# A fused attention and MLP kernel: two bf16 dummy products fewer in the head, and q's transposing transfers issued directly behind x's

## The chip, the cores and the metric

The kernel runs on one core of a Trainium2 chip. A core has five engines that run side by side, each with its own queue that it works off in order: PE (TensorE, matrix products), DVE (VectorE), ACT (ScalarE), POOL (GpSimd) and SP (SyncE, which here only issues transfers). Data moves between the chip's memory and the core's working memory (SBUF) by transfers that run on 16 DMA engines; in this kernel SP, POOL and, at the very end, ACT issue them. Products are written to PSUM, of which there are eight banks. The metric is the device time of one execution in microseconds (us). Where a row of the profile says PEld, it is PE loading the stationary operand of a product.

## The reference

The inputs are q, k and v of shape (8, 8, 576, 64), that is 8 batches of 8 heads, 576 rows and 64 columns; a scale of 64 numbers; and two weight matrices. All are float32.

```python
kv = np.einsum('bhsd,bhse->bhde', k, v)
out = np.einsum('bhsd,bhde->bhse', q, kv)
rms = np.sqrt(np.mean(out * out, axis=-1, keepdims=True) + 1e-06)
attn = out / rms * g_norm
x = attn.transpose(0, 2, 1, 3).reshape(4608, 512)
h = x @ w_in                        # 512 -> 2048
g = np.where(h > 0.0, h, np.exp(np.minimum(h, 0.0)) - 1.0)
return g @ w_out                    # 2048 -> 512
```

It is an attention without softmax: one 64x64 matrix kv per head and batch, a product of q with it, and a normalisation of each row. An MLP with the ELU function follows. The result is float32 of shape (4608, 512).

## The kernel before

**Tiling.** The rows are worked in nine pieces T. Pieces 0 to 7 take the first 512 rows of each batch; piece 8 takes the last 64 rows of all eight batches. Each piece has an attention part, which makes x (512 rows, stored with the model dimension on the partitions, `xT`), and an MLP part. The MLP has two halves: `mm1(T, i)` for i = 0 to 7 makes two 128-wide strips of h with eight 128x512 products (line 466), and ACT and DVE turn them into `gT` (lines 478 to 497); `mm2(T, j, f0, f1)` makes a part of the output for a quarter j of the rows (line 513), ACT copies it to `o_sb` (line 526), and SP stores two quarters at a time (line 535).

**Order.** The order of work on each engine is the order in which the program is written; nothing reorders it. Where an instruction needs another engine's result it waits, and whatever is behind it on its engine waits too.

**The head (lines 550 to 761).** Before the first MLP can run, batch 0 goes through attention with a path of its own. `idle(ps, n, dtype)` (line 599) issues n products of a block of zeros into a PSUM bank that nobody reads: dummy products. They stand in four places: two in float32 and one in bf16 at the start (lines 609 and 610), one in float32 behind the first transposes of q (line 633), and one in bf16 between the score products and the kv products of the third and fourth quarter of the heads (line 729). Behind them come, quarter by quarter, kv (`kv_first`, line 174), scores (`se_first`, line 653), squares on ACT (line 662), their mean by a product with a constant matrix (`mean_first`, line 665), logarithm and exponential on ACT (lines 668 and 671), and a scaling on DVE (`scale_first`, line 674). `first` (line 683) then starts the first MLP on the quarters that are ready. k, v, both weight matrices and most of q are loaded by POOL's queue, with the cast to bf16 in the transfer (lines 104, 118, 136 and 142).

**The groups (function `group`, line 832).** From piece 2 on, the loop at line 900 runs one group per piece T. It holds the MLP's first half of piece T, pieces of the second half of T - 1, and the attention of T + 1. In step i = 0 stands kv of T + 1, in step 3 the scores, in step 4 (for T = 2: in steps 2 and 4) the scaled rows `xs`, and for each half of them a transposing transfer on SP, `xd0` and `xd1` (line 325), which writes x. A last scaling by g, `xg0` and `xg1` (line 332), runs on DVE in steps 6 and 7 (for T = 2: 5 and 6). The first product of the next group reads x.

**The q path.** For pieces 2 to 8, q also has to be transposed. The steps for a batch b are: `fetch(b)` (line 821) issues on POOL the loads of q, k and v; POOL unpacks q into `q_bf` by four copies (line 150), the last of which waits for v to land (line 132); then SP issues one transposing transfer from `q_bf` to `qT`, called `qd` (`q_dma`, line 251, issue in line 255). Before POOL fetches the batch after next, it runs a one-element copy, `landed` (lines 124 and 428), that waits until qT has landed; in the profile this is `gate<-qT` in line 125. So group T starts with `landed` of T + 1 and `fetch(T + 2)`, and its last statement is `ahead["qd"]()` for T + 2. For batch 2 and batch 3 `qd` is called ahead of the loop (lines 811 and 878). Piece 8 has its q loaded by SP (line 89) and cast by POOL.

So SP's order in a group from T = 3 on is: store, `xd0`, `xd1`, store, `qd`. Tiles for `qT`, `q_bf`, packed q, k and v exist twice, `o_sb` three times.

Of the kernel before, what the change touches and what calls it, by code (L numbers as in the profile page):

```python
# [16 lines left out]
def kernel(  # L17
# [16 lines left out]
    B, H, S, D = q.shape  # L34
# [8 lines left out]
    NT = B + 1  # L43
# [401 lines left out]
    def mm1(T, i, cols=(slice(0, 512),), relu=False, home="m1", between=(), by_c=False):  # L445

        if i == 0:
            gT[T] = mlpg.tile([P, FC, G], BF16, name="gT", tag="gT")
        x = xT[T]
        if home == "m2":  # L450
            h_ps = [ps_m2.tile([P, G], FP32, name="h_ps", tag="mm2") for _ in range(2)]
            parts = [(a, a + 1, h_ps[a].rearrange("p (a t) -> p a t", a=1)) for a in range(2)]
        else:
            if home == "at":
                both = at_tile(FP32).rearrange("p (a t) -> p a t", a=2)
            else:
                both = ps_m1.tile([P, 2, G], FP32, name="h_ps", tag="mm1")
            h_ps = [both[:, a, :] for a in range(2)]
            parts = [(0, 2, both)]
        for cs in cols:  # L460
            steps = [(a, c) for a in range(2) for c in range(KC)]
            if by_c:
                steps.sort(key=lambda step: step[1])
            for a, c in steps:
                f = 2 * i + a
                nc.tensor.matmul(  # L466
                    h_ps[a][:, cs],
                    lhsT=w_in_sb[:, c, f * P : f * P + P],
                    rhs=x(c, cs),
                    start=(c == 0),  # L470
                    stop=(c == KC - 1),
                )
        return elu(T, i, parts, relu, between)
# [34 lines left out]
    def mm2(T, j, f0, f1, hold=False):  # L508

        if f0 == 0 and (T, j) not in o_ps:  # L510
            o_ps[T, j] = ps_m2.tile([P, DM], FP32, name="o_ps", tag="mm2")
        for f in range(f0, f1):
            nc.tensor.matmul(  # L513
                o_ps[T, j],
                lhsT=gT[T][:, f, j * P : j * P + P],
                rhs=w_out_sb[:, f, :],
                start=(f == 0),
                stop=(f == FC - 1),
            )
        if f1 == FC and not hold:  # L520
            mm2_out(T, j)
# [74 lines left out]
    def bank(n):  # L596
        return ps_head.tile([P, G], FP32, name=f"bank{n}", tag=f"bank{n}")

    def idle(ps, n, dtype=BF16):
        z = zeros.bitcast(dtype)  # L600
        for _ in range(n):
            nc.tensor.matmul(ps, lhsT=z[:, 0:P], rhs=z[:, 0:512], start=True, stop=True)
# [4 lines left out]

    idle_ps = bank(1)
    idle(idle_ps, 2, FP32)
    idle(idle_ps, 1)  # L610
    q_st = q_raw0.rearrange("p u (l s j d) -> p u s j l d", l=2, s=2, j=J)
    q_two = attp.tile([P, NPAIR, J, 2, D], BF16, name="q_two", tag="q_two", bufs=1)
    qT0 = attp.tile([P, NPAIR, G], BF16, name="qT", tag="qT")
# [29 lines left out]
    def kv_first(c):  # L643
        u, l = c // 2, c % 2
        kv_single(0, kv_ps, u, (l,))
        ls = slice(l * 64, l * 64 + 64)
        nc.vector.tensor_copy(out=kv0[ls, u], in_=kv_ps[ls, :, u * 64 : u * 64 + 64])
# [19 lines left out]
    def log_first(c):  # L667
        nc.scalar.activation(r0[c], mean0[c], AF.Ln, bias=eps_col)
# [4 lines left out]
    def scale_first(c):  # L673
        nc.vector.scalar_tensor_tensor(
            out=x0[:, c, :], in0=se0[c], scalar=g_col, in1=r0[c], op0=ALU.mult, op1=ALU.mult
        )
# [43 lines left out]
    mean0[1] = bank(0)  # L720
    mean_first(1)
    log_first(1)
    idle_ps = bank(3)
    se0[2] = bank(1)
    se_first(2)
    square_first(2)
    exp_first(1)
    scale_first(0)
    idle(idle_ps, 1)
    kv_first(3)  # L730
    mean0[2] = bank(2)
    mean_first(2)
# [33 lines left out]
    at, ahead = attention(1), attention(2)  # L766
# [54 lines left out]
    def fetch(b):  # L821
        if b < B:
            fetch_packed_q(b)
            packed_kv(b)
            for name in "kv":
                fetch_packed_kv(name, b)
            unpack_q(b, Q)
        else:
            fetch_q(B)
            cast_q(B, Q)  # L830

    def group(T, at, lead, second, relu=()):

        for piece in lead:
            mm2(T - 1, *piece)
        if T == 2:
            for i in range(8):
                n = i // 2 - 1
                early = [at[f"sum{n}"], at[f"inv{n}"]] if i in (2, 4) else ()
                rest = mm1(T, i, relu=i in relu, between=early)  # L840
                for piece in second.get(i, ()):
                    mm2(T - 1, *piece)
                if i in (2, 4):
                    at[f"mul{n}"]()
                rest()
                if i in (2, 4):
                    at[f"xd{n}"]()
                if i == 0:
                    at["kv"]()
                if i in (1, 3):  # L850
                    at["se"]({i // 2: None})
                    at[f"sq{i // 2}"]()
                if i in (5, 6):
                    at[f"xg{i - 5}"]()
            return
        for i in range(8):
            between = [at["sq1"], at["sum0"], at["inv0"], at["sum1"]] if at and i == 4 else ()
            rest = mm1(T, i, relu=i in relu, between=between)
            if at and i == 3:
                at["se"]({0: None, 1: [ps_m2.tile([P, DM], FP32, name="se_ps", tag="mm2") for _ in range(2)]})  # L860
                at["sq0"]()
            for piece in second.get(i, ()):
                mm2(T - 1, *piece)
            if at and i == 4:
                at["inv1"]()
                for n in range(2):
                    at[f"mul{n}"]()
                    at[f"xd{n}"]()
            rest()
            if at and i == 0:  # L870
                at["kv"]()
            if at and i > 5:
                at[f"xg{i - 6}"]()

# [2 lines left out]
    at, ahead = ahead, attention(3)  # L877
# [22 lines left out]
    for T in range(2, NT):  # L900
        at = ahead if T + 1 < NT else None
        if T + 2 < NT:
            at["landed"]()
            fetch(T + 2)
            ahead = attention(T + 2)
        if T == 2:
            lead, pieces, steps = [], [(2 + i // 4, 4 * (i % 4), 4 * (i % 4) + 4) for i in range(2, 8)], range(1, 7)
        elif T < B:
            lead, pieces, steps = halves[:1], halves[1:], (0, 1, 2, 4, 5, 6, 7)
        else:  # L910
            lead, pieces, steps = halves[:1], halves[1:], range(7)
        second = {i: [piece] for i, piece in zip(steps, pieces)}
        group(T, at, lead, second, {2: (1, 2, 4, 5), B: ()}.get(T, (4, 5)))
        if T + 2 < NT:
            ahead["qd"]()
    rows = out.rearrange("(i l s) f -> l s i f", l=2, s=S)
    pieces = [(j, slice(0, DM)) for j in range(J - 1)]
# [46 lines left out]
```

## Time and profile before

Four runs of the kernel took 283.79 to 284.12 us, with a median of 283.96 us.

| | |
|---|---|
| time of the profiled execution | 283.96 us |
| its span, first to last instruction | 282.2 us |
| PE busy | 275.0 us (97%) |
| DVE busy | 161.7 us (57%) |
| ACT busy | 152.9 us (54%) |
| POOL busy | 58.5 us (21%) |
| mean granted clock of PE | 0.998 |
| transfers issued by SP and ACT, share of the 16 DMA engines | 24.2% |
| transfers issued by POOL, share of the 16 DMA engines | 40.5% |
| line 325, x's transposing transfers | 12, landing 3.2 us after issue |
| line 255, q's transposing transfers | 7, landing 4.5 us after issue |
| line 125, POOL's waits for qT | 6, 60.9 us in all |

How to read it: the span is the stretch that the profiler covers, and the run's time has some 1.8 us around it. A row of the timeline has the start, the length, the engine, the line of the kernel, the operation, what it writes and reads, how many instructions are merged into it, and in brackets how long the engine stood idle before it and what released it. The end of a product in a row is modelled, so products overlap in the rows; the distance between their starts is the time that they take. `SPq` rows are SP issuing transfers.

### The profile page before, as it was taken

The page shows a single profiled execution, that of the slowest core. Times are in us where ns is not written, and L with a number is a line of the kernel's source. Part 1 is how long each engine was busy: PE and PEld are TensorE (multiplying, and loading weights), DVE is VectorE, ACT ScalarE, POOL GpSimd, SP SyncE. Part 2 cuts the span into 40 slices and gives each one's busy share as a digit, 9 for nine tenths or more (in the row PEclk, how much of TensorE's full clock was granted, in tenths as well). Part 3 has the DMA queues.
Part 4 walks back from the last instruction along what each step waited for, and adds up shares of the span by engine and source line. Part 5 has one row for each costly group of instructions (what it writes and reads, how often), then busy time and mean ns, then how long its engine had stood idle before and what let it go on. Part 6 is the DMA issues. An engine that isn't in the chain of part 4 may idle for free.

```text
span 282.2 us, 5134 instructions
## 1 busy us (share of the span) xinstructions
PE 275.0 (97%) x2118; PEld 129.3 (46%) x2118; DVE 161.7 (57%) x233; ACT 152.9 (54%) x220; POOL 58.5 (21%) x102
## 2 busy tenths in 40 slices
PE   7799999999999999999999999999999999999994
PEld 3434554445444444444444444444444444444444
DVE  3449643988388646843693468445854586444400
ACT  3669446666487438533863377237923692333311
POOL 7843722152421241005110421012000000000000
PEclk9999999999999999999999999999999999999999
DMA  7999999696996695358945794354236123010122
GB/s 195 198 200 202 206 202 194 177 189 108 200 178 90 153 188 129 74 149 123 195 78 145 96 222 79 110 125 142 53 95 77 74 41 111 0 74 2 75 74 74
DMA packets 57579, 35.98 MB, mean 128 GB/s; under 512 B 32852, under 2 KB 55124, under 8 KB 57556
## 3 DMA queue, kind: packets, MB, share of 16 engines
q0 software_dynamic: 21808, 17.30, 40.5%
q1 hardware_dynamic: 35348, 17.83, 24.2%
q10 hardware_dynamic: 400, 0.52, 0.6%
q8 instruction: 16, 0.26, 0.4%
q14 instruction: 7, 0.06, 0.1%
HBM read 36.70 MB, written 9.44 MB: 164 GB/s over the span
## 4 chain that ended last, share of the span: by engine, by line
PE 92%; DMA 5%; POOL 1%; ACT 0%; issue 0%; DVE 0%; POOLq 0%
PE h_ps L466 42%; PE o_ps L513 39%; PE o_ps L923 5%; DMA w_in_sb<-in_moe_w_in_dram 3%; DMA k_pk<-in_k_dram 2%; PE at L174 2%; PE at L466 1%; PE at L200 1%; PE bank L683 1%; POOL w_in_sb L136 1%; PE se_ps L200 1%; ACT qT L248 0%; PE at L184 0%; PE se_ps L412 0%; DVE qT L249 0%
## 5 line engine op out<-in xcount | busy, mean ns | idle before, releaser
L466 PE MATMUL h_ps<-xT,w_in_sb 128*128 128x512 bf16 x536 | 125.7, 379 | 0.0
L513 PE MATMUL o_ps<-w_out_sb,gT 128*128 128x512 bf16 x512 | 120.5, 379 | 0.0
L478 ACT ACTIVATE elu_e<-h_ps 128x1024 bf16<-128x1024 f32 (+1 forms) x71 | 70.0, 995 | 80.6 <-PE h_ps L466 77.8
L466 PEld LDWEIGHTS <-w_in_sb 128*128 128x128 bf16 x552 | 52.5, 98 | 63.2 <-DVE xT L332 1.7
L513 PEld LDWEIGHTS <-gT 128*128 128x128 bf16 x512 | 49.5, 98 | 58.3
L489 DVE TENSOR_SCALAR elu_e<-elu_e 128x1024 bf16<-128x1024 bf16 (+1 forms) x75 | 33.1, 441 | 73.8 <-ACT elu_e L478 73.8
L497 DVE TENSOR_TENSOR gT<-elu_e,h_ps 128x1024 bf16<-128x1024 bf16 (+1 forms) x51 | 60.1, 1179 | 5.3
L526 ACT COPY o_sb<-o_ps 128x512 f32<-128x512 f32 x32 | 18.6, 586 | 15.5 <-PE o_ps L513 15.5
L217 DVE TENSOR_REDUCE ss<-sq 128x16 f32<-128x1024 bf16 x16 | 19.4, 1219 | 7.6 <-ACT sq L212 6.9
L150 POOL COPY q_bf<-q_pk 128x512 bf16<-128x512 bf16 x28 | 17.0, 637 | 23.7 <-DMA q_pk<-in_q_dram 23.7
L484 ACT ACTIVATE elu_h<-h_ps 128x1024 bf16<-128x1024 f32 (+1 forms) x20 | 19.5, 990 | 0.0
L497 DVE TENSOR_TENSOR gT<-elu_e,elu_h 128x1024 bf16<-128x1024 bf16 x20 | 14.1, 703 | 2.3 <-ACT elu_h L484 0.8
L923 PE MATMUL o_ps<-w_out_sb,gT 128*128 128x512 bf16 (+1 forms) x80 | 14.1, 337 | 0.0
L125 POOL COPY gate<-qT 1x1 bf16<-1x1 bf16 x6 | 1.1, 182 | 60.9 <-DMA qT<-q_bf 60.9
L104 POOL DMA_DIRECT2D q_pk<-in_q_dram x14 | 10.6, 758 | 4.0 <-issue 1.8
L228 DVE TENSOR_TENSOR xs<-at,ss 128x512 bf16<-128x512 f32 x16 | 10.2, 682 | 1.2 <-ACT ss L224 1.2
L923 PEld LDWEIGHTS <-gT 128*128 128x128 bf16 x80 | 7.7, 98 | 6.4 <-DVE gT L497 0.4
L212 ACT ACTIVATE sq<-at 128x1024 bf16<-128x1024 f32 x9 | 9.4, 1043 | 1.6 <-PE at L200 1.0
L118 POOL DMA_DIRECT2D k_pk<-in_k_dram x12 | 8.3, 691 | 3.1 <-DMA w_in_sb<-in_moe_w_in_dram 1.5
L118 POOL DMA_DIRECT2D v_pk<-in_v_dram x12 | 8.2, 684 | 2.9 <-DMA w_out_sb<-in_moe_w_out_dram 1.8
L174 PEld LDWEIGHTS <-k_pk 64*64 64x64 bf16 x576 | 6.5, 107 | 5.1 <-issue 4.6
L931 ACT COPY o_last<-o_ps 128x512 f32<-128x512 f32 (+1 forms) x5 | 2.5, 501 | 10.8 <-PE o_ps L923 10.8
(79 smaller groups left out, 138.6 us busy)
## 6 DMA issues: line engine op xcount, KB each, us to landing
out_dram<-o_sb SPq DMA_DIRECT2D x16, 512.0 KB, 3.8
q_pk<-in_q_dram POOLq DMA_DIRECT2D x14, 256.0 KB, 5.5
k_pk<-in_k_dram POOLq DMA_DIRECT2D x6, 576.0 KB, 8.5
v_pk<-in_v_dram POOLq DMA_DIRECT2D x6, 576.0 KB, 11.4
w_in_sb<-in_moe_w_in_dram POOLq DMA_DIRECT2D x5, 256.0 KB, 8.5
st_q<-in_q_dram SPq DMA_DIRECT2D x2, 512.0 KB, 5.5
w_out_sb<-in_moe_w_out_dram POOLq DMA_DIRECT2D x2, 512.0 KB, 13.7
w_out_sb<-in_moe_w_out_dram POOLq DMA_DIRECT2D x4, 256.0 KB, 11.3
```

The lines of the kernel that those rows point to most:

```text
L118: nc.gpsimd.dma_start(out=raw[name, b].rearrange("p h j d -> p h (j d)")[:, hs], in_=in_[:, hs])
L150: eng.tensor_copy(out=out_, in_=in_)
L174: nc.tensor.matmul(kv_ps[l * 64 : l * 64 + 64, s, u * 64 : u * 64 + 64], lhsT=bf["k", T][rows, j, 2 * u + l, :], rhs=bf["v", T][rows, j, 2 ...
L217: nc.vector.reduce_sum(out=ss, in_=sq.rearrange("p c (h e) -> p (c h) e", h=H), axis=AX.X)
L466: nc.tensor.matmul(h_ps[a][:, cs], lhsT=w_in_sb[:, c, f * P : f * P + P], rhs=x(c, cs), start=(c == 0), stop=(c == KC - 1),)
L478: nc.scalar.activation(e[:, lo:hi, :], ps, AF.Exp)
L484: nc.scalar.activation(h[:, lo:hi, :], ps, AF.Relu)
L489: nc.vector.tensor_scalar(out=e[:, lo:hi, :], in0=e[:, lo:hi, :], scalar1=1.0, scalar2=1.0, op0=ALU.min, op1=ALU.subtract,)
L497: nc.vector.tensor_tensor(out=gT[T][:, 2 * i + lo : 2 * i + hi, :], in0=e[:, lo:hi, :], in1=h, op=ALU.add if relu else ALU.max,)
L513: nc.tensor.matmul(o_ps[T, j], lhsT=gT[T][:, f, j * P : j * P + P], rhs=w_out_sb[:, f, :], start=(f == 0), stop=(f == FC - 1),)
L526: nc.scalar.copy(o_sb[T][:, j % 2, :], o_ps.pop((T, j)))
L923: nc.tensor.matmul(ps, lhsT=gT[B][:, f, j * P : j * P + P], rhs=w_out_sb[:, f, cols], start=(f == 0), stop=(f == FC - 1),)
```

## The change

Two calls of `idle` are taken out, each one bf16 product of 128x128 by 128x512 zeros: the third dummy at the start, and the one in front of the last quarter's kv, together with the PSUM bank that it was written to. The float32 dummies stay.

The call of `qd` at the end of a group stays only for T = 6, where T + 2 is piece 8. For the groups T = 2 to 5 it moves into `group`, behind step 5, so that the transfer for batch T + 2 is issued behind `xd1` of step 4. SP's order in these groups becomes: store, `xd0`, `xd1`, `qd`, store. The calls for batches 2 and 3 ahead of the loop are as before. The order of POOL, DVE and ACT is unchanged.

```diff
     idle_ps = bank(1)
     idle(idle_ps, 2, FP32)
-    idle(idle_ps, 1)
     q_st = q_raw0.rearrange("p u (l s j d) -> p u s j l d", l=2, s=2, j=J)
...
     log_first(1)
-    idle_ps = bank(3)
     se0[2] = bank(1)
     se_first(2)
     square_first(2)
     exp_first(1)
     scale_first(0)
-    idle(idle_ps, 1)
     kv_first(3)
...
                 if i == 0:
                     at["kv"]()
+                if i == 5:
+                    ahead["qd"]()
                 if i in (1, 3):
...
             rest()
             if at and i == 0:
                 at["kv"]()
+            if i == 5 and T + 2 < B:
+                ahead["qd"]()
             if at and i > 5:
                 at[f"xg{i - 6}"]()
...
         group(T, at, lead, second, {2: (1, 2, 4, 5), B: ()}.get(T, (4, 5)))
-        if T + 2 < NT:
+        if T + 2 == B:
             ahead["qd"]()
```

## The prediction

> **What bounds the kernel now.** I read the page first, then the chain that ended last, then the timeline of the head, and last the timelines of SP and POOL around the transfers that move.
>
> The page says that TensorE is the only full engine:
>
> ```profile
> span 282.2 us, 5134 instructions
> ...
> PE 275.0 (97%) x2118; PEld 129.3 (46%) x2118; DVE 161.7 (57%) x233; ACT 152.9 (54%) x220; POOL 58.5 (21%) x102
> ```
>
> The chain, in order of time, says from when it is full. Before 17.48 us the chain is a transfer, w_in_sb; behind it, up to 278.58, there are PE rows with one exception, two evacuations of qT at 33.26:
>
> ```profile
> 8.92 8.51 DMA w_in_sb<-in_moe_w_in_dram
> 17.43 0.05 issue
> 17.48 0.82 PE bank L683 x3
> ...
> 264.66 13.92 PE o_ps L923 x80
> ```
>
> So the time is "third chunk of w_in landed" + "products behind it" + a tail of stores. An edit counts only if it moves 17.48, or makes a gap in PE behind it. Seven L683 products take 1.51 us in the chain, 0.216 each.
>
> The timeline of the head holds both removed products, each the 128x512 bf16 kind:
>
> ```profile
> 4.94 0.38 PE L602 MATMUL bank<-zeros 128*128 128x512 bf16 x1
> ```
>
> ```profile
> 4.97 0.62 PEld L621 LDWEIGHTS <-q_two 128*128 128x128 bf16 x8 [0.61 <-DVE q_two L150]
> ...
> 7.91 0.47 PE L174 MATMUL kv_ps<-v_pk,k_pk 64*64 64x64 bf16 x18 [0.92 <-DMA v_pk<-in_v_dram]
> ...
> 12.12 0.39 PE L602 MATMUL bank<-zeros 128*128 128x512 bf16 x1
> 12.44 0.36 PEld L174 LDWEIGHTS <-k_pk 64*64 64x64 bf16 x18 [0.23 <-issue]
> ...
> 13.12 0.38 PE L665 MATMUL bank<-sq,means 128*128 128x512 bf16 x1 [0.21 <-ACT sq L662]
> ...
> 16.65 0.75 DVE L674 SCALAR_TENSOR_TENSOR xT<-bank,g_col,r 128x512 bf16<-128x512 f32 x1 [0.64 <-ACT r L671]
> ```
>
> And the end of the group that runs batch 3's MLP, where SP and DVE meet:
>
> ```profile
> 114.03 2.61 SPq L325 DMA_TRANSPOSE xT<-xs  x2
> ...
> 121.85 0.34 SPq L535 DMA_DIRECT2D out_dram<-o_sb  x1
> 122.24 0.48 DVE L332 TENSOR_SCALAR xT<-xT,g_col 128x1024 bf16<-128x1024 bf16 x1
> 122.28 2.58 SPq L255 DMA_TRANSPOSE qT<-q_bf  x1
> 122.77 1.41 PEld L466 LDWEIGHTS <-w_in_sb 128*128 128x128 bf16 x8 [0.34 <-DVE xT L332]
> ...
> 126.83 0.18 POOL L125 COPY gate<-qT 1x1 bf16<-1x1 bf16 x1 [17.07 <-DMA qT<-q_bf]
> ```
>
> L332 ends at 122.72 and the next group's first product starts at 122.78: the one place in a group where PE has no reserve.
>
> **The change, part by part.** *First dummy product* (0.22 us: 4.94 to 5.16). Without it the transposes start when their cast lets them, 4.97 plus some 0.1, so about 0.1 us earlier. The cover is the landing of v_pk: PE waits 0.92 us for it and starts kv at 7.91, whatever came before. Nothing.
>
> *Second dummy product* (0.32 us: 12.12 to 12.44). kv of the last quarter starts up to 0.32 earlier. What is late next is ACT: the mean product of 13.12 waits for a square that ACT ends at 13.07, and ACT is 100% busy from 11 to 15 us in the windows. The following cast on DVE (12.96) can start only when the scaling of 11.98 to 12.73 is done, so the score product of 13.43 gains 0.1 at most, and its square waits for ACT until 14.12 all the same. The first L683 product (13.76) waits for w_in. Then 17.43 stands. Nothing; were the cover gone it would be 0.32.
>
> *Four transposing q transfers* (batches 4 to 7; the call for batch 3 ahead of the loop and that for batch 8 stay). On SP each is 2.6 us of issue, and goes from behind one store of o_sb to ahead of it, directly behind x's second half. Does it wait there, with the store queued behind it? It needs q_bf: POOL's last copies end at 87.53, 109.76, 142.18 and 171.46; x's second issue ends at 88.81, 116.64, 146.20 and 174.93. It is ready by 1.3 to 6.9 us, more where the fetch comes earlier. The store of 121.85 finds SP free at 119.3; that of 91.06 waits until about 91.5, with three o_sb buffers behind it. Nothing.
>
> x's halves land 3.2 us after issue: the second, issued at about 115.35, at 118.5, and L332 takes it at 122.24. Were its remaining 1.9 us doubled by q's packets, 120.4: still in time. In batch 2's group the second half is issued about 87.55, lands at 90.7, at worst 92.6; L332 would end at 93.1, and PE wants it at 93.65. Nothing.
>
> The gate on POOL opens with qT's landing, 4.55 us after issue: at about 121.2 instead of 126.83 (and 150.4 for 156.00, 179.5 for 185.19; 93.4 for 96.03). Then POOL issues four loads, 3.0 us, and they run 5.6 us earlier (2.6 for batch 5). Their buffers are free by then: kv and unpacking of the batch two before are long done. Batch 8's sixteen loads on SP also start 2.6 us earlier, at about 180.5, and its casts with them. PE waits for none of these loads today, and earlier is no loss.
>
> What is new is where POOL's load issues fall: about 121.7 to 124.7, across L332 at 122.24. Do these two engines hinder each other? The trace has both answers. L489, of like kind, takes 0.43 alone, but
>
> ```profile
> 57.10 0.62 DVE L489 TENSOR_SCALAR elu_e<-elu_e 128x1024 bf16<-128x1024 bf16 x1 [0.73 <-ACT elu_e L478]
> 57.45 0.76 POOL L118 DMA_DIRECT2D k_pk<-in_k_dram  x1
> ```
>
> with an issue ending 0.37 us after its start (+0.19); 0.47 at 130.04 and 0.51 at 159.17 with 0.22 and 0.26 to go (+0.04, +0.08); and 0.43 at 96.63, inside an issue with 0.74 to go (0). By my estimate L332 starts 0.2 us before an issue ends: +0.06. It falls on PE in full, but at two group starts only, 122.76 and 151.9: the group after has no POOL loads (batch 8 comes over SP), and at 93.65 the gate opens later than L332. Sum +0.12 us; ends 0 and 2 x 0.19 = 0.38. Below nothing I see no reason: L332 cannot start before L497 of the last step.
>
> The Trainium skill (SBUF — State Buffer, section "SBUF: two separate sides") calls the port pair of VectorE and GpSimd an exclusive lock, held for the whole instruction, whose loser fully blocks. That speaks against this change: by it L332 could lose up to a whole issue, 0.75 us, twice, and the sum would be +1.5. The rows at 96.63 (no loss) and 57.10 (0.19) show less, and they decide.
>
> Sum: 0 + 0 + 0 + 0.12. The profiled execution took 283.96 us, span 282.2 and 1.76 around it; it is the median of the four runs itself. Forecast 284.1.
>
> **The rivals.** *The clock falls in the head* (slower). The dummies keep PE busy, and PE was not at full rate at first: float32 products start 0.85 us apart (2.50, 3.35, 4.21), then 0.73, then bf16 ones 0.22 apart. If the last spacing is part slow, part twice as fast, the change is at 4.82. At the end it goes back: granted clock 0.62 over 281.0 to 282.2 is a fall to 0.5 at 281.29, 2.7 us after the last product. Which share of busy time keeps the clock? In the 3.4 us before 281.29 PE was busy 0.7 us (20%) and it fell; from 4.82 to 8.23 it was busy 2.47 us by the windows (72%) and it stayed. Without the first dummy that is 66%; the second takes 90% to 81% in a later stretch. If the bound lies anywhere between 20 and 72, the chance to cross it is 6 in 52, one in ten. The price: 1.9 us of products from 8.23 to 11.64 (8 transposes at 0.056, two score and two mean products at 0.22, two kv rows at 0.28 without their last product's tail) take twice as long; x's last quarter (17.40) has 0.73 us until PE wants it at 18.13; so 0 to 1.2 us for one such stretch, 3.4 for two. I take +1.0: 285.0. It decides only when the loss exceeds 0.73.
>
> The Trainium skill (TensorE: Matmul & The Clock Gate, section "The HAM clock gate") has a free-running window of 3413 ns and half clock after an idle one; 281.29 - 4.82 is 81 of them to the hundredth, so the rule holds here, and an idle window by its words the head never has: +0 by the page.
>
> *The dummies are on the path* (faster). For it: they stand in line on PE, 0.22 + 0.32 = 0.54 us, 283.4. Against it: both waits for DMA behind them. It would need w_in to land earlier too.
>
> *x lands late.* If q's packets delay x's second half past L332 by more than the 0.5 us left at 93.1, or 3.7 at the others, PE waits one for one: some +0.5 in one group, 284.5; a collision dearer than the rows above (0.38, 284.3) ends in the same place.
>
> *The transfers do not move.* SP's order shows each one place earlier, but were q_bf late they would start as before: 284.0.
>
> **How the numbers follow.** 0.2%, 0.57 us, is about what a measurement of this kernel can tell from no change. Forecast, with the transfers that do not move: 0.66, all within. Clock: 0.12, of it 0.10 slower. x late or dearer collision: 0.12, half of it slower. Dummies on the path: 0.06, half of it faster; 0.04 for what I don't see, half each way. Faster 0.05, same 0.77, slower 0.18. The range leaves out the dearer half of the clock case and what is unseen: 283.4 (both dummies) to 285.0.
>
> **What would show it.** L602 with six records, w_in still landing at 17.4 and the first c=3 products at 18.1: dummies hidden. SP's L255 near 88.9, 116.7, 146 and 175, the gate near 93.4, 121.2 and 150.4: the move did what it says. L332 at 122.24 with 0.48 to 0.67 us, PE behind it late by the excess. L174 rows of 0.47 us growing to 0.6 or more, or transposes 0.11 apart behind 8.2 us, would make me wrong through the clock; w_in landing at another time, through something that I hold constant.

## The result, and the profile after

The changed kernel took 284.27 us in the median of 37 runs (283.35 to 285.25), the kernel before 283.93 us in 61 (283.27 to 284.73). The ratio is 1.0015, with a 95% interval of 1.0009 to 1.0022: a loss of some 0.4 us (0.34 between the medians, 0.43 between the means) that is clear of noise, and smaller than the 0.2% that the prediction took as its bound.

The profiled execution of the changed kernel shows no loss at all. Its page begins so:

```profile
span 281.9 us, 5130 instructions
...
PE 275.0 (98%) x2116; PEld 129.5 (46%) x2116; DVE 161.7 (57%) x233; ACT 152.9 (54%) x220; POOL 59.0 (21%) x102
```

PE is busy as long as before, with two products fewer, and the span is 0.3 us shorter. So one profiled execution does not hold the answer. The list of all executions does. For each of them the mean granted clock of TensorE, its share of full speed, is recorded, and the values are not spread evenly: they lie between 0.997 and 1.000, or at 0.993 to 0.994.

| kernel | executions | at 0.994 or below | mean of these | mean of the others |
|---|---|---|---|---|
| changed kernel | 38 | 15 | 284.80 us | 284.02 us |

(The 38 are the 37 runs and the profiled one.) Fifteen of 38 times 0.78 us is 0.31 us, most of what was lost. For the kernel before, this measurement has the times alone, without the clock of each execution.

The timeline of the head of the changed kernel, with the lines that answer to those of before (line numbers differ by one to three):

```profile
5.06 0.93 PE L620 MATMUL bank<-ident,q_two 128*128 128x128 bf16 x8
...
7.73 0.47 PE L174 MATMUL kv_ps<-v_pk,k_pk 64*64 64x64 bf16 x18 [0.28 <-DMA v_pk<-in_v_dram]
...
12.09 0.47 PE L174 MATMUL kv_ps<-v_pk,k_pk 64*64 64x64 bf16 x18
...
12.95 0.38 PE L664 MATMUL bank<-sq,means 128*128 128x512 bf16 x1 [0.39 <-ACT sq L661]
...
13.59 1.25 PE L682 MATMUL h_ps<-xT,w_in_sb 128*128 128x512 bf16 x4
...
14.68 0.38 PE L664 MATMUL bank<-sq,means 128*128 128x512 bf16 x1
...
16.48 0.75 DVE L673 SCALAR_TENSOR_TENSOR xT<-bank,g_col,r 128x512 bf16<-128x512 f32 x1 [0.64 <-ACT r L670]
...
19.34 5.34 PE L466 MATMUL h_ps<-xT,w_in_sb 128*128 128x512 bf16 x24
```

The transposes start 0.10 us earlier and kv still waits for v_pk. The last scaling comes 8.75 us behind the first kv, as before (7.91 to 16.65: 8.74). The second dummy's slot on PE turned into a longer wait for ACT in front of the mean product, 0.39 instead of 0.21 us.

SP, POOL and DVE at the end of the group that runs batch 3's MLP, from SP's own timeline and from that of a window around the group's end:

```profile
113.61 2.61 SPq L325 DMA_TRANSPOSE xT<-xs  x2
116.32 1.69 SPq L255 DMA_TRANSPOSE qT<-q_bf  x1
```

```profile
120.25 0.37 POOL L125 COPY gate<-qT 1x1 bf16<-1x1 bf16 x1 [13.79 <-DMA qT<-q_bf]
...
120.71 1.49 POOL L104 DMA_DIRECT2D q_pk<-in_q_dram  x2
...
121.82 0.63 DVE L332 TENSOR_SCALAR xT<-xT,g_col 128x1024 bf16<-128x1024 bf16 x1
122.18 0.76 POOL L118 DMA_DIRECT2D k_pk<-in_k_dram  x1
122.50 0.55 PEld L466 LDWEIGHTS <-w_in_sb 128*128 128x128 bf16 x4 [0.48 <-DVE xT L332]
```

The transfer moved, POOL issues its loads across L332, and L332 takes 0.63 us instead of 0.48. In the chain that ended last the next group's eight products take 1.89 us there, against 1.75 before.

### The profile page after: what moved, and what is told of

Same layout as the page of the kernel before. It is cut to its first block, busy times and chain, and to the rows that moved or that the text cites. A ratio compares the mean times of both kernels' runs of the same rounds, so it can differ in the third digit from the quotient of the medians.

```text
span 281.9 us, 5130 instructions
## 1 busy us (share of the span) xinstructions
PE 275.0 (98%) x2116; PEld 129.5 (46%) x2116; DVE 161.7 (57%) x233; ACT 152.9 (54%) x220; POOL 59.0 (21%) x102
## 4 chain that ended last, share of the span: by engine, by line
PE 85%; DMA 11%; POOL 2%; issue 1%; ACT 0%; POOLq 0%
PE h_ps L466 39%; PE o_ps L513 36%; DMA w_out_sb<-in_moe_w_out_dram 9%; PE o_ps L924 5%; DMA k_pk<-in_k_dram 2%; POOL w_in_sb L136 2%; PE at L174 2%; PE at L200 1%; PE at L466 1%; PE se_ps L200 1%; PE se_ps L412 0%; POOL v_pk L118 0%; PE xt_ps L304 0%; PE at L304 0%; POOL kv_sb L766 0%
## 5 line engine op out<-in xcount | busy, mean ns | idle before, releaser
L466 PE MATMUL h_ps<-xT,w_in_sb 128*128 128x512 bf16 x536 | 125.7, 379 | 0.0
L466 PEld LDWEIGHTS <-w_in_sb 128*128 128x128 bf16 x552 | 52.5, 98 | 63.4 <-DVE xT L332 1.8
L125 POOL COPY gate<-qT 1x1 bf16<-1x1 bf16 x6 | 1.8, 296 | 55.6 <-DMA qT<-q_bf 55.6
```

The source lines that it names most:

```text
L466: nc.tensor.matmul(h_ps[a][:, cs], lhsT=w_in_sb[:, c, f * P : f * P + P], rhs=x(c, cs), start=(c == 0), stop=(c == KC - 1),)
```

## The experiments

Two theories stood against each other. A: the loss is the clock of TensorE, which in some executions falls to one half for one stretch of 3.4 us, because without a dummy the head has too little work for PE. B: the loss is q's order. The counts below take a mean granted clock of 0.994 or less as the sign of a fall: 3.41 us at half rate are 1.7 us of 282, 0.006.

**Each part alone.** The first dummy out:

```diff
     idle(idle_ps, 2, FP32)
-    idle(idle_ps, 1)
```

> Only the first bf16 dummy product (behind the two float32 ones at the start) is taken out; the second dummy and q's transfers stay as before. Theory A (the loss of 0.34 us is the clock of TensorE, which falls for one stretch of 3.4 us in some executions, because a removed dummy leaves a stretch of the head too idle; a mean granted clock of 0.994 is such a fall, since 3.4 us at half rate are 1.7 of 282 us): the stretch that thins out most without this product lies between 3 and 8 us, where 0.22 us of 3.4 go and the share stays above 0.6, so hardly any execution at 0.994 more than before, and 283.9 +- 0.15. Theory B (the loss is the order of q's transfers alone): no difference to before, 283.9. If this dummy alone makes the falls: 283.9 + 0.3.

Measured: 0.9995 (0.9986 to 1.0003), none of 11 executions at 0.994, mean 283.64 us.

The second dummy out:

```diff
-    idle_ps = bank(3)
     se0[2] = bank(1)
...
     scale_first(0)
-    idle(idle_ps, 1)
```

> Only the second bf16 dummy product (ahead of the last quarter's kv) is taken out. Theory A: the starts of the products give a busy share of 0.45 to 0.50 instead of 0.54 to 0.59 for stretches of 3.4 us that end between 12.4 and 14.8 us, so about 4 executions in 10 have a granted clock of 0.994 and some +0.75 us each; the median 284.2 (+0.3), with the other executions at 283.9. Theory B: no difference to before, 283.9.

Measured: 1.0019 (1.0005 to 1.0033). Six of 12 executions at 0.994 or below, with a mean of 284.95 us; the other six 283.74.

Only q's order, both dummies in (the diff of the change without its first two hunks):

> Both dummies stay; only the four transposing transfers of q are issued behind x's. Theory A: executions at 0.994 as rare as before; what is left is the lengthened L332 at one or two group starts, 0.15 us at each in the profile after, so 284.0 to 284.2 (+0.1 to +0.3). Theory B: the whole loss, 284.3 (+0.34), in executions of every granted clock.

Measured: 0.9999 (0.9990 to 1.0008), no execution at 0.994. The 0.1 to 0.3 us that L332 was expected to add is not seen in the times. One of its 11 took 1014 us; it is like no other, its cause is not known, and the means leave it out.

The changed kernel again:

> The changed kernel itself, for a profile and for the granted clock of each execution beside that of the kernel before on the same chip. Theory A: 4 executions in 10 at 0.994 with a mean of 284.8, the others at 284.0; 284.3 in the median. If the profile falls on one at 0.994, it shows products at double distance for 3.4 us between 8 and 16 us. Theory B: 284.3, and executions of the kernel before at 0.994 as often as here.

Measured: 1.0006 (0.9995 to 1.0017). Three of 12 at 0.994, mean 284.77; the other nine 283.78. The kernel before, on the same chip: none of 35, mean 283.83. The share was 3 in 12 here and 15 in 38 before; what a median of the changed kernel shows depends on how many falls it catches.

B falls: q's order alone costs nothing that the times can tell, and with the second dummy alone taken out the falls are there, at a cost like that of the whole change.

**Is it the share of busy time, or the place of the product?** The changed kernel, with one dummy put back into a gap, where PE waits for ACT anyway:

```diff
     kv_first(3)
+    idle(bank(3), 1)
     mean0[2] = bank(2)
```

> The changed kernel with one bf16 dummy product put back, but behind the last quarter's kv instead of ahead of it, where TensorE waits 0.39 us for ACT's square in the profile after. Theory A (the busy share of a stretch of 3.4 us decides whether the clock falls): the place does not matter, the share is back at 0.54 or more; no execution at 0.994, 283.8 (as the changed kernel's other executions, 283.8 to 284.0). Theory C (not the share: the product ahead of kv did something by its place, such as holding back the kv products): executions at 0.994 as often as without it, some 4 in 10, and 284.3.

Measured: 1.0007 (0.9998 to 1.0015), none of 11 at 0.994, mean 283.88. The falls are gone though the product stands elsewhere, so its old place is not what matters.

The second dummy at half and at a quarter of its columns:

```diff
-    idle(idle_ps, 1)
+    nc.tensor.matmul(
+        idle_ps[:, 0:256], lhsT=zeros[:, 0:P], rhs=zeros[:, 0:256], start=True, stop=True
+    )
```

> The kernel before with the second dummy product cut from 512 to 256 columns, 0.11 us instead of 0.22. Theory A, with a bound in the share that lies between the valley without the product (0.45 to 0.50) and with it (0.54 to 0.59): the phases of the stretch for which it falls get fewer; executions at 0.994 in 0 to 3 of 10, median 283.8 to 284.1. As many as without it (4 in 10) would put the bound above the half product's share, none below it.

Measured: 0.9991 (0.9983 to 1.0000), none of 11 at 0.994, mean 283.52.

> The kernel before with the second dummy product cut to 128 columns, 0.05 us. Theory A, bound in the busy share of the stretch that ends near 13.2 us: with 256 columns none of 11 executions was at 0.994, without it 34 of 74 or so with and without the other edits were near 4 in 10. If the bound lies midway, 1 to 2 of 11; 283.5 to 283.9. As many as without the product (4 to 5 of 11, 284.1) would put the bound between the shares of 128 and 256 columns, a step of 0.016.

Measured: 1.0005 (0.9995 to 1.0014), one of 11 at 0.994 (284.50); the others 283.78. One of 11 can't be told from none, and is few beside the executions without the product.

**A fall seen.** Both dummies out, q's order as before:

> Both dummies out, q's transfers as before. Theory A: as the changed kernel, without its 0.1 to 0.17 us at one group start: 4 executions in 10 at 0.994 with a mean of 284.8, the others at 283.7; about 284.1 in the mean. If q's order took part in the falls, none at 0.994 and 283.7.

Measured: 1.0019 (1.0005 to 1.0033), six of 12 at 0.994 with a mean of 284.81; the other six 283.85. And the profiled execution is one of them. The windows of this kernel, whose columns are the stretch, its length, the busy time of PE, PEld, DVE, ACT and POOL with their instructions, the granted clock, and the share and rate of the DMA engines:

```profile
12.00:13.00 1.00, 0.57 (x19) 0.45 (x18) 0.81 (x2) 1.00 (x3) 1.00 (x2) 1.00 1.44 195
13.00:14.00 1.00, 1.00 (x4) 0.26 (x4) 0.60 (x1) 1.00 (x3) 0.65 (x2) 0.59 1.46 197
14.00:15.00 1.00, 1.00 (x3) 0.29 (x2) 0.15 (x1) 1.00 (x3) 0.37 (x1) 0.50 1.45 197
15.00:16.00 1.00, 1.00 (x4) 0.41 (x3) 0.75 (x1) 0.01 (x1) 0.74 (x1) 0.50 1.49 209
16.00:17.00 1.00, 1.00 (x5) 0.38 (x4) 0.00 (x0) 0.84 (x2) 0.65 (x1) 0.70 1.40 186
17.00:18.00 1.00, 1.00 (x7) 0.42 (x5) 0.49 (x1) 0.48 (x1) 0.09 (x1) 1.00 1.45 196
```

A mean of 0.59 in the second row is a fall to 0.50 at 13.18; 0.70 in the fifth is the return at 16.60: 3.42 us. The kernel before, in the same windows, has a clock of 1.00 throughout, and PE with the dummy in the first row:

```profile
12.00:13.00 1.00, 0.91 (x21) 0.55 (x20) 0.78 (x2) 1.00 (x3) 1.00 (x2) 1.00 1.45 196
13.00:14.00 1.00, 0.88 (x5) 0.23 (x5) 0.63 (x2) 1.00 (x3) 0.54 (x2) 1.00 1.46 197
```

The products ahead of the fall, from the timeline of PE in the kernel with both out:

```profile
9.63 0.38 PE L664 MATMUL bank<-sq,means 128*128 128x512 bf16 x1
10.11 0.41 PE L652 MATMUL bank<-qT,kv 64*64 64x512 bf16 x2
10.59 0.47 PE L174 MATMUL kv_ps<-v_pk,k_pk 64*64 64x64 bf16 x18
11.27 0.38 PE L664 MATMUL bank<-sq,means 128*128 128x512 bf16 x1 [0.20 <-ACT sq L661]
11.57 0.40 PE L652 MATMUL bank<-qT,kv 64*64 64x512 bf16 x2
12.05 0.47 PE L174 MATMUL kv_ps<-v_pk,k_pk 64*64 64x64 bf16 x18
12.90 0.38 PE L664 MATMUL bank<-sq,means 128*128 128x512 bf16 x1 [0.39 <-ACT sq L661]
```

And what the fall costs, from the timeline of the same kernel:

```profile
13.78 1.89 PE L682 MATMUL h_ps<-xT,w_in_sb 128*128 128x512 bf16 x4
...
15.46 0.63 PE L664 MATMUL bank<-sq,means 128*128 128x512 bf16 x1
...
16.13 0.69 ACT L667 ACTIVATE r<-bank,eps_col 128x512 f32<-128x512 f32 x1 [1.12 <-PE bank L664]
...
17.51 0.75 DVE L673 SCALAR_TENSOR_TENSOR xT<-bank,g_col,r 128x512 bf16<-128x512 f32 x1 [1.72 <-ACT r L670]
...
20.56 0.81 PE L466 MATMUL h_ps<-xT,w_in_sb 128*128 128x512 bf16 x3
```

Four products ahead of the last mean product take twice their time; the mean comes at 15.46 instead of the 14.68 of the profile after, ACT waits 1.12 us for it, the last scaling is 1.03 us later and L466 begins at 20.56 instead of 19.34.

The second dummy out once more:

> The kernel without the second dummy once more, for a profile of an execution at 0.994. Theory A: if the profile is of such an execution, the products of one stretch of 3.41 us that begins between 12.4 and 14.8 us stand at double distance (0.43 us for 512 columns), and the first product of the second MLP piece starts about 1 us later than in the others; a stretch elsewhere, or none, is against A. Times: 4 to 5 in 10 at 0.994 and 284.9, the others at 283.7.

Measured: 1.0004 (0.9993 to 1.0016), four of 12 at 0.994 with a mean of 284.48, the others 283.62. Its profile was of one of the others, so it says nothing on where a fall lies; the one fall in a profile is that of the kernel above.

All counts together:

| second dummy | kernels | at 0.994 or below |
|---|---|---|
| out | changed kernel (twice), second out (twice), both out | 34 of 86 |
| 128 columns | quarter | 1 of 11 |
| 256 columns | half; half with the first out | 0 of 22 |
| 512 columns | first out, q's order only, in the gap | 0 of 33 |

The kernel before had none at 0.993 or 0.994 among the 91 executions timed beside these; one took 293.64 us at 0.948, another kind of event that I cannot explain. These counts carry the cause, not the medians: two of the five measurements without the product (1.0006 and 1.0004) can't be told from the kernel before, as fewer falls came up in them. In the four of the five that were timed beside these 91, the executions that did not fall lie within 0.15 us of the kernel before, so what is lost is lost in the falls.

**The longer L332.** To see whether POOL's load issues make it longer, POOL also waits for L332 before it fetches, from group 4 on; q's order is moved, both dummies are in:

```diff
             at["landed"]()
+            if T > 2:
+                after(xT[T](0, slice(None))[0:1, 2, 0:1])
             fetch(T + 2)
```

> Only q's order moved, both dummies in, and POOL's fetch from group 4 on also waits for the last scaling of x (L332), so that POOL issues its loads behind it. If the longer L332 and the gap at the start of that group come from POOL's load issues beside it, L332 is back at 0.48 us (0.58 to 0.65 in the three profiles with moved transfers) and the first product of that group starts 0.22 to 0.23 us behind the one before (0.32 to 0.39 there). If they come from the transfers themselves, both stay long. The time, 283.8, can't tell 0.15 us in one look.

Measured: 283.91 us in one execution. The end of the same group in the timeline:

```profile
122.15 0.48 DVE L332 TENSOR_SCALAR xT<-xT,g_col 128x1024 bf16<-128x1024 bf16 x1
122.68 1.41 PEld L466 LDWEIGHTS <-w_in_sb 128*128 128x128 bf16 x8 [0.34 <-DVE xT L332]
...
122.75 0.18 POOL L125 COPY gate<-xT 1x1 bf16<-1x1 bf16 x1 [1.80 <-DVE xT L332]
123.20 1.50 POOL L104 DMA_DIRECT2D q_pk<-in_q_dram  x2 [0.27 <-issue]
```

With POOL's issues behind it L332 is back at 0.48. In the profiles with moved transfers and no such wait it took 0.63 (after), 0.65 (q's order only), 0.58 (changed kernel again) and 0.68 us (dummy in the gap). So the collision is real, some 0.1 to 0.2 us once per execution, at the first of the two group starts only. The wait holds back the loads themselves along with their issuing, so this run clears q's moved transfers but does not part POOL's issuing from the traffic of the loads.

**A better version?** The first out, the second at 256 columns:

> The first dummy taken out and the second cut to 256 columns, q's transfers as before: what the runs so far point to. Theory A: no execution at 0.994, since the stretch near 13.2 us keeps its 256 columns, and the 0.1 to 0.25 us that each of the two edits gave alone: 283.4 to 283.6, the ratio 0.998 to 0.9995. If taking both products' time out does not add up, as 283.5 to 283.7.

Measured: 0.9997 (0.9988 to 1.0006), none of 11 at 0.994, mean 283.59. No kernel here beats the one before by more than its interval; the half dummy alone comes nearest, with 1.0000 at its upper end.

## Why the prediction was right, and where it was not

The forecast was 284.1, the measurement 284.27, in the range and on the side that it gave. That the number came so near is luck: the sum's only cost, 0.12 us at L332, cannot be seen in the times, and what moved the median is the clock, a rival that had a chance of 0.12 and was priced as if it came in every execution.

*First dummy, nothing.* Right: alone 0.9995 (0.9986 to 1.0003), and kv waits for v_pk with or without it.

*Second dummy, nothing.* Right for the time on the path: the last scaling stands 8.7 us behind the first kv either way, and in the profile with both dummies and POOL's later gate L466 starts at 19.42, against 19.34 without them. Wrong as a whole, since the product's work was not in its time: without it 34 of 86 executions had a fall of the clock and were 0.8 to 1.2 us longer, with it none of 33. This is the step that failed.

*w_in's landing sets the head.* True of the profile that I had and of two others (L466 at 19.78 with q's order only, at 20.21 with the quarter dummy), not of most. In the changed kernel's profile the third chunk was there before PE came to it, and L466 began at 19.34 instead of 20.07. The profile gave one execution's value for something that changes from one to the next by up to 0.9 us.

*Four q transfers, nothing.* Right: 0.9999 (0.9990 to 1.0008). They were issued at 88.56, 116.32, 147.09 and 174.74, near the 88.9, 116.7, 146 and 175 foreseen. The gate opened at 120.25 rather than 121.2, as the issue took 1.69 us there and not the 2.6 that it took right behind a store.

*L332, 0.06 at each of two group starts.* Mechanism right, size off: 0.15 at the first in the profile after, where POOL's issue had 0.38 us to go and not the 0.2 of my estimate (the row with 0.37 to go had shown +0.19); nothing at the second, where the gate opened at 151.15 and the loads were issued behind L332. The sum, 0.15, met the 0.12, but the times could not tell it from nothing. The lock as the Trainium skill states it (SBUF — State Buffer, section "SBUF: two separate sides") would have cost up to 0.75 at each by the prediction's estimate; the rows show a fifth of that, at one of the two.

*The clock.* The rival named the mechanism, the price (+1.0; measured +0.8 to +1.2 between the two kinds of execution of one kernel) and the sign, and got a chance of 0.12. Two things made that too small. I measured the share of busy time by the page's busy columns, in which the end of a product is modelled: 90% to 81% around the second dummy. Counted by the distances between starts it is another number. In the 3.41 us ahead of the fall at 13.18 there are two pairs of score products and two mean products of 0.22 each, two kv rows of 0.30 and 0.07 of an earlier mean product: 1.54 us, 0.45. With 128 columns more it is 0.47, with 256 it is 0.48, with 512 it is 0.51. The twelve other profiles did not fall in the head; counted the same way, over stretches laid end to end from the rise of the clock, the emptiest in the head of any of them, from 9.14 to 12.55 in the profile after, is 0.52 busy. So the profiles put the bound between 0.45 and 0.52; the runs with 256 columns (none of 22) put it below 0.48 if their executions lay their stretches like the one that fell, which is not shown. And I laid the stretches where one execution had them, at 4.82 and every 3.41 us after that; in the execution that fell they ended at 13.18, which is 6.36 and two times 3.41, and a stretch that ends there is among the emptiest of its head. In the traces of the twelve profiles without a fall the granted clock rose earlier, at 4.50 to 5.72 us. So a fall is not a yes or no of the kernel but a chance per execution, 34 in 86. That the other falls lie at the same place as the one seen is argued from their clock and their cost, not shown; and since the ends that leave less than 0.48 busy, about 12.8 to 13.4, are a fifth of 3.41 us and falls were 4 in 10, the count does not yet explain how often they come.

The rule of the Trainium skill that I set against the trace for this (TensorE: Matmul & The Clock Gate, section "The HAM clock gate") holds in its length, 3413 ns (here 13.18 to 16.60), and in its free-running phase (a rise at 4.82 in one profile and 6.36 in another). Its idle window I read as one without work, and so +0; a stretch with 0.45 of work was idle enough.

*x late, dummies on the path, transfers that do not move.* None was seen: x's scalings ran at their places, and in eight of the nine profiles without a fall in which w_in came in time L466 starts at 19.33 to 19.49, with both products, with one, with half of one or with none; in the ninth, the one with the dummy in the gap, everything from kv on was later, and L466 starts at 19.78.

## What to carry to other kernels

A product that nobody reads may be there for the clock: before taking it out, add up the products' real time, by the distances between their starts, over every stretch as long as the one by which the clock changes (3.41 us here), wherever it may begin, and not only at the one that the profile happens to show. When a loss is a chance per execution, one profile can miss it; look at the granted clock of every execution. In a gap where its engine waits anyway a dummy product cost nothing here that the times can tell (1.0007, 0.9998 to 1.0015), and half of one did as well as a whole one.

## What the runs showed of the hardware

- The granted clock of TensorE fell to one half after a stretch of 3.41 us that was 0.45 busy, and came back 3.42 us later; in no profile did it fall in the head after a stretch that was 0.52 busy or more. With a product of 256 columns put back, 0.48 by the same count, none of 22 executions fell.
- When the stretches begin differs between executions of one kernel. The distances of the first float32 products show the clock rising near 4.8 us in the first profile of the kernel before, and the fall at 13.18 puts it near 6.36 in the kernel with both out.
- A product of zeros keeps the clock up: one of 512 columns, 0.22 us, took the falls from 34 in 86 to 0 in 33.
- q's transposing transfer takes longer to issue right behind a store: 2.56 to 2.62 us (five of the kernel before), against 1.67 to 2.15 behind x's transposing transfer (four of the changed kernel) and 1.58 where SP's last store was 15 us back (at 69.30 before).
- A 128x1024 scaling on DVE (L332) takes 0.48 us alone and 0.58 to 0.68 across the end of a load issue on POOL. In the profile of the changed kernel again it also took 0.90 once, at 90.03, beside a copy on POOL.
